# Pairs of heads in one 4 MB tile, and five rows per partition for the weights, in a decode-attention and MLP gradient kernel

## The chip, the cores and the metric

The kernel runs on one core of a Trainium2 chip. The metric is the device time of one execution in microseconds. Times of single instructions, transfers and packets come from one profiled execution; the trace counts from its first instruction.

## The reference

One token (a row of 640) passes a layer norm, then attention over a cache of 8192 positions and a gated MLP in parallel. What is computed is the output and, by the chain rule, the gradients of it against all inputs but one for a given `grad_out`:

```python
xn = layernorm(x)                                   # (1, 640)
q = (xn @ wq).reshape(32, 128)                      # 32 heads of 128
s = einsum("hd,hkd->hk", q, k_cache) * 128 ** -0.5  # k_cache, v_cache: (32, 8192, 128) bf16
p = softmax(s)
o = einsum("hk,hkd->hd", p, v_cache)
out_0 = x + o.reshape(4096) @ wo + (silu(xn @ w1) * (xn @ w3)) @ w2    # F = 1728
# gradients: out_1 dx, out_2 dK, out_3 dV, out_4 dwq, out_5 dwo, out_6 dw1, out_7 dw3, out_8 dw2
```

With one query per head, dV of a head is the outer product of p and a row (wo times grad_out), and dK the outer product of U = p * (v . do - sum) and q. So each head reads K and V of 2 MB each and writes dK and dV of 2 MB each: 268 of the 303.5 MB that move.

## The kernel before

A tile of K or V of one head lies as 128 partitions of 64 positions: `(p j) d -> p (j d)`, 16 KB of consecutive memory per partition. Ten such tiles (`free_slots`, `kv_tiles`) are all the space for K and V. The gradients are written into the tile of the input: `outer_v` puts dV over V, `outer_k` puts dK over K, `store` sends the tile out and hands it back.

All these transfers are issued on SP (SyncE) in the order of the program (`fifo`). A transfer waits on SP for what it needs, and everything behind it on SP waits too. `load_next` takes the next of `pending` (K0, V0, K1, V1 and so on) and the tile that has been free the longest, but only when at least `lag` tiles are free (1 at the start, 3 afterwards), so that the store which last used the tile has some time to finish:

```python
        if not pending or len(free_slots) < lag[0]:
            return
```

It is called after every store and whenever the MLP gives back a tile. Loads and stores of wq, wo and their gradients in groups of four heads go over POOL's queue (q0), those of group 0, of the last group and a few rows of others over SP (q1).

`head(h)` is an order written out by hand. TensorE transposes K in chunks of 8 position rows (`T`, four 128x128 transposes, evicted by ScalarE to a `KT` tile), `Mp` multiplies pairs of chunks with the query spread in `qz`, `ev` evicts the scores, `selm` selects and transposes them into the tile `m`. Then `mx`, `mx_bc`, `expo`, `zsum` and `probs` make the softmax; each is a small step on another engine. The same is done with V (`rdot`, `dsum` make U). `o_sum` and `dq_sum` are weighted sums over V and K on TensorE with the weights spread in `Z`. VectorE writes the outer products of head h-1 while TensorE works on head h: `outers_a(h-1)` at the start of `head(h)` (two halves of dV, its store, the first half of dK), `outers_b(h-1)` after `probs(h)` (the rest of dK, its store). `side_k`, `side_m`, `side_v`, `side_pe1` and others place the work of the groups (`prep_do`, `prep_q`, `fin_wo`, `fin_wq`) between these steps.

Before head 2 the kernel does the MLP (`mlp`, `MLP_AT = 2`). Its weights lie in four of the ten tiles, w1 and w3 as `(ci p) f`, so that a partition holds the rows p, p + 128, ...; four of the five blocks lie in `mA` and `mB`, the fifth in `mC`. The gradients dw1 and dw3 are written over the weights and leave over POOL's queue, and each tile then goes back to `free_slots`. For dx the products of weights and the gradient row (`L657`, `L670`) are summed over columns on TensorE into `dx_acc`.

At the end comes the last group's dwo and dwq, the layer norm's gradient, and out_1, transposed to five rows of 128 and sent in two transfers.

Of the kernel before, what the change touches and what calls it, by code (L numbers as in the profile page):

```python
# [16 lines left out]
P = 128  # L17
# [4 lines left out]
def kernel(  # L22
# [31 lines left out]
    GH = 4  # L54
    NG = H // GH
    GW = GH * DH
    KVN = J * DH
# [16 lines left out]
    kc = A_k_cache.rearrange("b h (p j) d -> (b h) p (j d)", p=P)  # L74
    vc = A_v_cache.rearrange("b h (p j) d -> (b h) p (j d)", p=P)
    dkc = out_2.rearrange("b h (p j) d -> (b h) p (j d)", p=P)
    dvc = out_3.rearrange("b h (p j) d -> (b h) p (j d)", p=P)
    wq_v = A_wq.rearrange("(ci p) n -> p ci n", p=P)
    wo_v = A_wo.rearrange("(h p) c -> p h c", p=P)
    dwq_v = out_4.rearrange("(ci p) n -> p ci n", p=P)  # L80
    dwo_v = out_5.rearrange("(h p) c -> p h c", p=P)
    w1_v = B_w1.rearrange("(ci p) f -> p ci f", p=P)
    w3_v = B_w3.rearrange("(ci p) f -> p ci f", p=P)
    dw1_v = out_6.rearrange("(ci p) f -> p ci f", p=P)
    dw3_v = out_7.rearrange("(ci p) f -> p ci f", p=P)
# [5 lines left out]
    NA = NC - 1  # L91
    NSLOT = 10
    RW = 64
# [22 lines left out]
    free_slots = [kvpool.tile([P, KVN], BF16, name=f"kv{i}", tag=f"kv{i}") for i in range(NSLOT)]  # L116
    kv_tiles = {}
    pending = [("K", h) if k == 0 else ("V", h) for h in range(H) for k in range(2)]

    lag = [1]  # L120

    def load_next():
        if not pending or len(free_slots) < lag[0]:
            return
        kind, h = pending.pop(0)
        t = free_slots.pop(0)
        fifo(t[:], (kc if kind == "K" else vc)[h])
        kv_tiles[(kind, h)] = t
# [5 lines left out]
    mC = free_slots.pop(0)  # L134
    mD = free_slots.pop(0)
    mA = free_slots.pop(0)
    mB = free_slots.pop(0)
    w1a = mA[:, 0:NA * F].rearrange("p (c f) -> p c f", f=F)
    w3a = mB[:, 0:NA * F].rearrange("p (c f) -> p c f", f=F)
    w1b = mC[:, 0:F]  # L140
    w3b = mC[:, F:2 * F]
    w2b = mC[:, 2 * F:2 * F + (NB - NBA) * D].rearrange("p (b c) -> p b c", c=D)
    BC0 = 2 * F + (NB - NBA) * D
    assert BC0 + 2 * F <= KVN
    bc_sb = mC[:, BC0:BC0 + 2 * F].rearrange("p (w f) -> p w f", f=F)
    w2a = mD[:, 0:NBA * D].rearrange("p (b c) -> p b c", c=D)
# [6 lines left out]
    fifo(w1a, w1_v[:, 0:NA, :])  # L153
    fifo(w1b, w1_v[:, NA, :])
    fifo(w3a, w3_v[:, 0:NA, :])
    fifo(w3b, w3_v[:, NA, :])
    for _ in range(2):
        load_next()
# [8 lines left out]
    pm_one = masks[:, 0:2]  # L167
    nc.vector.memset(pm_one[:, 0:1], 1.0)
    nc.vector.memset(pm_one[:, 1:2], -1.0)
    ones_b = pm_one[:, 0:1].to_broadcast([P, P])  # L170
    negones_b = pm_one[:, 1:2].to_broadcast([P, P])
    one_bf = consts.tile([P, 1], BF16, name="one_bf")
    nc.vector.memset(one_bf[:], 1.0)
    eps_t = consts.tile([P, 1], F32, name="eps_t")
    nc.vector.memset(eps_t[:], LN_EPS)
# [18 lines left out]
    DHALF = D // 2  # L194

# [7 lines left out]
    negmean = consts.tile([P, 1], F32, name="negmean")  # L203
    rstd = consts.tile([P, 1], F32, name="rstd")
    x_col = consts.tile([P, NC], F32, name="x_col")
    g_col = consts.tile([P, NC], F32, name="g_col")
    xn_col = consts.tile([P, NC], F32, name="xn_col")
# [12 lines left out]
    ln3 = consts.tile([P, 3], F32, name="ln3")  # L220
    xsum, sumsq, std = ln3[:, 0:1], ln3[:, 1:2], ln3[:, 2:3]
    ps_xg = pst()
    ps_g = pst()
    for ci in range(NC):
        nc.tensor.matmul(ps_xg[:, ci:ci + 1], lhsT=x_row[:, ci * P:(ci + 1) * P], rhs=one_bf[0:1, :],
                         start=True, stop=True)
        nc.tensor.matmul(ps_xg[:, NC + ci:NC + ci + 1], lhsT=g_row[:, ci * P:(ci + 1) * P], rhs=one_bf[0:1, :],
                         start=True, stop=True)
# [6 lines left out]
    nc.vector.tensor_copy(x_col[:], ps_xg[:, 0:NC])  # L235
    nc.vector.tensor_copy(g_col[:], ps_xg[:, NC:2 * NC])
    nc.vector.tensor_reduce(xsum, x_col[:], AX.X, ALU.add)
    nc.tensor.matmul(ps_xg[:, 16:17], lhsT=ones_b, rhs=xsum, start=True, stop=True)
    nc.vector.tensor_scalar(negmean[:], ps_xg[:, 16:17], -1.0 / D, None, ALU.mult)
    nc.vector.scalar_tensor_tensor(xn_col[:], x_col[:], negmean[:], x_col[:], ALU.add, ALU.mult, accum_out=sumsq)  # L240
    nc.tensor.matmul(ps_xg[:, 17:18], lhsT=ones_b, rhs=sumsq, start=True, stop=True)
    nc.scalar.activation(std, ps_xg[:, 17:18], ACTF.Sqrt, bias=eps_t[:], scale=1.0 / D)
    nc.vector.reciprocal(rstd[:], std)
    nc.vector.tensor_scalar(xn_col[:], x_col[:], negmean[:], rstd[:], ALU.add, ALU.mult)
    nc.vector.tensor_copy(xn_col_bf[:], xn_col[:])

    def prep_new(g):
        G_ = grp[g]
        G_["cb"] = wpool.tile([P, 2, GH], BF16, name="cb", tag="cb")
        G_["do"] = wpool.tile([P, GH], F32, name="do_c", tag="do_c")  # L250
        G_["cm"] = wpool.tile([P, 2, 2, GH, 2], BF16, name="cm_g", tag="cm_g")
        G_["od"] = wpool.tile([P, GH, 2], F32, name="od_g", tag="od_g")

    def prep_do(g, hh):
        G_ = grp[g]
        junk = small.tile([P, D], BF16, name="side", bufs=1)
        nc.vector.scalar_tensor_tensor(junk[:], G_["wo"][:, hh, :], 1.0, g_bc[:], ALU.mult, ALU.mult,  # L257
                                       accum_out=G_["do"][:, hh:hh + 1])
        if hh == GH - 1:
            nc.vector.tensor_copy(G_["cb"][:, 1, :], G_["do"][:])  # L260
# [18 lines left out]
    def prep_sel(g, ps):  # L279
        for par in range(2):  # L280
            nc.tensor.matmul(ps[:, par * 2 * GH:(par + 1) * 2 * GH], lhsT=sel[:, par, :],
                             rhs=grp[g]["cb"][:].rearrange("p a h -> p (a h)"), start=False, stop=True,
# [8 lines left out]
    NCH = J // 8  # L291
    QL = NCH - 2
    qz_tiles = []
    for i in range(2):
        qz = consts.tile([P, QL + 4 * QW], BF16, name=f"qz{i}")
        nc.vector.memset(qz[:], 0.0)
        qz_tiles.append(qz)
    P2_1 = consts.tile([P, J, 2], BF16, name="P2_1")
    U2_1 = consts.tile([P, J, 2], BF16, name="U2_1")
    NI = J // 4  # L300
    Z = consts.tile([P, QW - 4 + NI * QW], BF16, name="Z")
    nc.vector.memset(Z[:], 0.0)
    Z_vals = Z[:, QW - 4:].rearrange("p (i n) -> p i n", n=QW)[:, :, 0:4]
    QH = 2 * QW
    selc = consts.tile([P, QH], F32, name="selc")
    for x in range(QW // NCH):
        nc.vector.tensor_copy(
            selc[:, 2 * NCH * x:2 * NCH * (x + 1)].rearrange("p (e o t) -> p o e t", o=2, t=2),
            ident_f[:, 0:QH].rearrange("p (o x e t) -> p x o e t", o=2, e=NCH // 2, t=2)[:, x])

    def new_head(h):
        hd[h] = dict(kt={}, qz=qz_tiles[h % 2])

    def T(h, kind, c):
        W3 = kv_tiles[(kind, h)][:].bitcast(F32).rearrange("p (i w) -> p i w", w=P)
# [5 lines left out]
        hd[h]["kt"][(kind, c)] = KT  # L321

    def Mp(h, kind, c0):
        S_ = hd[h]
# [10 lines left out]
        for par in range(2):  # L335
            for c in (c0, c0 + 1):
                q = QW * (c - c0)
                o = QL + QW * (2 * a + par) - c0
                nc.tensor.matmul(S_[kind][q:q + QW, :], lhsT=S_["qz"][:, o:o + QW], rhs=KTb[c][:, par, :],  # L339
                                 start=(c0 == 0 and par == 0), stop=(c0 == NCH - 2 and par == 1),  # L340
                                 skip_group_check=True)

    def ev(h, kind):
        S_ = hd[h]
# [4 lines left out]
    def selm(h, kind):  # L349
        S_ = hd[h]  # L350
        if kind == "K":
            S_["m"] = ps_m.tile([P, 512], F32, name="m", tag="m")
        b0 = 0 if kind == "K" else J
        XS = S_.pop("xr" + kind)
        for k in range(4):
            nc.tensor.matmul(S_["m"][:, b0:b0 + 4 * J].rearrange("p (x c k t) -> p k x c t", x=4, k=4, t=2)[:, k],  # L356
                             lhsT=XS[0:QH, k, :], rhs=selc[0:QH].rearrange("p (x c t) -> p x c t", x=4, t=2),
                             start=(kind == "K" and k == 0), stop=True, is_transpose=True, skip_group_check=True)
        S_[kind] = S_["m"][:, b0:b0 + J]

    def fill_qz(h):
        g, hh = divmod(h, GH)
        nc.vector.tensor_copy(
            hd[h]["qz"][:, QL:QL + 4 * QW].rearrange("p (a t n) -> p a t n", t=2, n=QW)[:, :, :, 0:2],
            grp[g]["cm"][:, :, :, hh, :].rearrange("p t a m -> p a t m"))

    def rows_pe(h, ps, first):
        g, hh = divmod(h, GH)
        for a in range(2):
            nc.tensor.matmul(ps[:, a * DH:(a + 1) * DH], lhsT=grp[g]["cb"][:, a, hh:hh + 1].to_broadcast([P, P]),  # L370
                             rhs=ident_bf[:], start=(first and a == 0), stop=True, skip_group_check=True)
        hd[h]["ps_r"] = ps

    def rows_act(h):
        qd = small.tile([P, 2, DH], BF16, name="qd")
        nc.scalar.copy(qd[:].rearrange("p a d -> p (a d)"), hd[h].pop("ps_r"))  # L376
        hd[h]["qd"] = qd

    def mx(h):
        S_ = hd[h]  # L380
        S_["mrow"] = small.tile([P, 1], F32, name="mrow")
        nc.vector.tensor_reduce(S_["mrow"][:], S_["K"][:, 0:J], AX.X, ALU.max)  # L382

    def mx_bc(h):
        S_ = hd[h]
        nc.tensor.matmul(S_["m"][:, 2 * J:2 * J + P], lhsT=S_["mrow"][:].to_broadcast([P, P]), rhs=ident_f[:],  # L386
                         start=False, stop=True, is_transpose=True, skip_group_check=True)
# [510 lines left out]
```

## Time and profile before

| | |
|---|---|
| median of 3 runs | 729.37 us (729.15 to 729.87) |
| profiled execution, first to last instruction (span) | 727.5 us |
| median minus span | 1.9 us |
| TensorE / VectorE / ScalarE busy | 603.3 / 459.8 / 376.2 us (83 / 63 / 52%) |
| packets and bytes | 28625, 303.54 MB, 417 GB/s over the span |
| q1 (SP) / q0 (POOL), share of 16 engines | 90.5% / 8.5% |
| mean granted TensorE clock | 0.916 |

The execution's time holds the span and what lies before its first and after its last instruction; the median minus the span stands for that here. The profile's page shows the span in 40 slices, with the busy share of each engine and of the 16 DMA engines in tenths. A packet is what one DMA engine moves at a time: 16 KB for a row of K or V. Lines such as `L318` are lines of the kernel above; `T` is L314 to L321, the outer product L466.

### The profile page before, as it was taken

Reading aid. Unit: us, or ns where it says so; the run is one execution under the profiler, and the core shown is the slowest. Engines: PE = TensorE matmul, PEld = TensorE weight load, DVE = VectorE, ACT = ScalarE, POOL = GpSimd, SP = SyncE. Lnnn points to the kernel's source line nnn. Section 1 sums busy time; section 2 is a strip of 40 time slices with the busy share of each in tenths; the row PEclk is TensorE's granted clock in tenths of the full one; section 3 lists DMA queues with packets and bytes.
Section 4 is the critical chain, followed back from the end, with each engine's and each line's share of the span. In section 5 each row is a group of like instructions: output and inputs, shape, how many; then the busy total and the mean of one; then the engine's idle time right before and its main releaser. Section 6 shows DMA issues by size and latency. Waiting matters only on the chain.

```text
span 727.5 us, 12942 instructions
## 1 busy us (share of the span) xinstructions
PE 603.3 (83%) x5186; PEld 377.1 (52%) x5193; DVE 459.8 (63%) x811; ACT 376.2 (52%) x727; POOL 32.3 (4%) x48
## 2 busy tenths in 40 slices
PE   4989489999899989888897789878796988988930
PEld 2547366665565556555454456445554555545510
DVE  4169646688868776667565756457665666667581
ACT  3640746665666566545454546455463555655510
POOL 0010100000000000000010000000000000000000
PEclk9997799999999999989998989899998999999965
DMA  9999999999999999999999999999999999999995
GB/s 351 400 411 421 428 426 430 427 426 430 420 420 431 430 412 420 426 428 421 420 425 428 430 426 428 420 431 428 421 422 427 429 425 423 425 432 427 426 415 221
DMA packets 28625, 303.54 MB, mean 417 GB/s; under 512 B 3354, under 2 KB 5929, under 8 KB 11924
## 3 DMA queue, kind: packets, MB, share of 16 engines
q1 hardware_dynamic: 22578, 277.75, 90.5%
q0 software_dynamic: 5968, 24.94, 8.5%
q8 instruction: 41, 0.67, 0.4%
q14 instruction: 20, 0.16, 0.1%
q10 hardware_dynamic: 18, 0.01, 0.0%
HBM read 151.34 MB, written 151.34 MB: 416 GB/s over the span
## 4 chain that ended last, share of the span: by engine, by line
DMA 51%; PE 36%; DVE 7%; ACT 2%; issue 1%; SPq 0%; ACTq 0%; DVEq 0%
DMA kv<-in_A_v_cache_dram 20%; PE pT L318 17%; DMA out_dram<-kv 16%; DMA kv<-in_A_k_cache_dram 14%; PE sA L339 5%; PE dA L339 4%; PE X L433 3%; DVE kv L466 3%; PE m L356 2%; DMA wo_g<-in_A_wo_dram 2%; ACT KT L320 1%; PE gu_ps L561 1%; PE pT L266 1%; PE m L400 1%; ACT KT L346 0%
## 5 line engine op out<-in xcount | busy, mean ns | idle before, releaser
L320 ACT COPY KT<-pT 128x512 f32<-128x512 f32 x512 | 288.3, 588 | 227.9 <-PE pT L318 208.6
L318 PE MATMUL pT<-ident_f,kv 128*128 128x128 f32 x2048 | 308.2, 290 | 53.7 <-DMA kv<-in_A_v_cache_dram 24.2
L318 PEld LDWEIGHTS pT<-ident_f,kv 128*128 128x128 f32 x2048 | 237.4, 149 | 146.2 <-PE pT L318 51.8
L466 DVE TENSOR_TENSOR kv<-qd,U 128x4096 bf16<-128x4096 bf16 x64 | 146.0, 2284 | 0.0
L466 DVE TENSOR_TENSOR kv<-qd,P 128x4096 bf16<-128x4096 bf16 x64 | 143.6, 2285 | 0.0
L433 PE MATMUL X<-kv,Z 128*32 128x512 bf16 x1024 | 97.1, 413 | 1.8 <-DVE Z L450 1.8
L339 PE MATMUL dA<-KT,qz 128*32 128x512 bf16 x512 | 84.2, 408 | 0.0
L339 PE MATMUL sA<-KT,qz 128*32 128x512 bf16 x512 | 83.5, 406 | 0.0
L416 DVE SCALAR_TENSOR_TENSOR U<-m,P 128x64 bf16<-128x64 f32 x32 | 7.5, 233 | 87.4 <-PE m L356 87.4
L433 PEld LDWEIGHTS <-Z 128*32 128x32 bf16 x1024 | 33.2, 101 | 35.3 <-issue 8.7
L339 PEld LDWEIGHTS <-qz 128*32 128x32 bf16 x1024 | 29.5, 95 | 40.8 <-issue 38.3
L382 DVE TENSOR_REDUCE mrow<-m 128x1 f32<-128x64 f32 x32 | 7.1, 223 | 68.4 <-PE m L356 68.3
L356 PE MATMUL m<-selc,KT 64*128 64x64 f32 x256 | 30.5, 242 | 10.3 <-ACT KT L346 10.3
L356 PEld LDWEIGHTS m<-selc,KT 64*128 64x128 f32 x256 | 21.5, 144 | 33.2 <-ACT KT L346 22.1
L376 ACT CAST qd<-pT 128x256 bf16<-128x256 f32 x32 | 11.9, 372 | 39.9 <-DVE kv L466 28.7
L389 DVE TENSOR_REDUCE negM<-m 128x1 f32<-128x128 f32 x32 | 9.3, 292 | 33.0 <-PE m L386 33.0
L526 DVE SCALAR_TENSOR_TENSOR wq_g<-wq_g,side 128x512 bf16<-128x512 bf16 x40 | 27.3, 683 | 0.0
L257 DVE SCALAR_TENSOR_TENSOR side<-wo_g,g_bc 128x640 bf16<-128x640 bf16 x32 | 26.2, 819 | 1.3 <-DMA wo_g<-in_A_wo_dram 0.9
L448 DVE SCALAR_TENSOR_TENSOR U<-m,P 128x128 bf16<-128x128 f32 x32 | 11.4, 356 | 16.3 <-PE m L446 16.3
L406 DVE RECIPROCAL rZ<-m 128x1 f32<-128x1 f32 x32 | 5.3, 166 | 24.2 <-PE m L400 24.2
L346 ACT COPY KT<-dA 64x512 f32<-64x512 f32 x32 | 18.6, 582 | 3.7 <-PE dA L339 3.7
L346 ACT COPY KT<-sA 64x512 f32<-64x512 f32 x32 | 18.6, 581 | 2.1 <-PE sA L339 1.9
(162 smaller groups left out, 372.7 us busy)
## 6 DMA issues: line engine op xcount, KB each, us to landing
out_dram<-kv SPq DMA_DIRECT2D x64, 2048.0 KB
kv<-in_A_k_cache_dram SPq DMA_DIRECT2D x32, 2048.0 KB
kv<-in_A_v_cache_dram SPq DMA_DIRECT2D x32, 2048.0 KB
wq_g<-in_A_wq_dram POOLq DMA_DIRECT2D x7, 640.0 KB, 13.4
wo_g<-in_A_wo_dram POOLq DMA_DIRECT2D x7, 640.0 KB, 19.1
out_dram<-wo_g POOLq DMA_DIRECT2D x7, 640.0 KB, 14.4
kv<-in_B_w_dram SPq DMA_DIRECT2D x2, 1728.0 KB
out_dram<-kv POOLq DMA_DIRECT2D x2, 1728.0 KB, 23.5
```

The costliest lines, as they stand in the source:

```text
L257: nc.vector.scalar_tensor_tensor(junk[:], G_["wo"][:, hh, :], 1.0, g_bc[:], ALU.mult, ALU.mult, accum_out=G_["do"][:, hh:hh + 1])
L318: nc.tensor.transpose(pT[:, k * P:(k + 1) * P], W3[:, 4 * c + k, :], ident_f[:])
L320: nc.scalar.copy(KT[:].rearrange("p k w -> p (k w)"), pT[:])
L339: nc.tensor.matmul(S_[kind][q:q + QW, :], lhsT=S_["qz"][:, o:o + QW], rhs=KTb[c][:, par, :], start=(c0 == 0 and par == 0), stop=(c0 == NCH ...
L346: nc.scalar.copy(XS[0:QH].rearrange("p k w -> p (k w)"), S_.pop(kind)[0:QH, :])
L356: nc.tensor.matmul(S_["m"][:, b0:b0 + 4 * J].rearrange("p (x c k t) -> p k x c t", x=4, k=4, t=2)[:, k], lhsT=XS[0:QH, k, :], rhs=selc[0:Q ...
L376: nc.scalar.copy(qd[:].rearrange("p a d -> p (a d)"), hd[h].pop("ps_r"))
L389: nc.vector.tensor_reduce(S_["negM"][:], S_["m"][:, 2 * J:2 * J + P], AX.X, ALU.max, negate=True)
L433: nc.tensor.matmul(xg["X"][q:q + QW, :], lhsT=Z[:, o:o + QW], rhs=W[:, N4 * i:N4 * (i + 1)], start=(slot == 0 and i < 4), stop=(slot == NS ...
L448: nc.vector.scalar_tensor_tensor(S_["U2"][:], S_["V"][:, 0:J].unsqueeze(2).to_broadcast([P, J, 2]), S_["m"][:, OC + NS:OC + NS + 1], S_["P ...
L466: nc.vector.tensor_tensor(dst[:, lo * DH:hi * DH].rearrange("p (j a b) -> p j a b", a=DH // 2, b=2), vec.rearrange("p (a b) -> p a b", b=2 ...
L526: nc.vector.scalar_tensor_tensor(wq_g[:, ci, :], wq_g[:, ci, :], 1.0, dqb, ALU.mult, ALU.mult, accum_out=dxa[:, ci, g:g + 1])
```

## The change

Heads 0, 1, 30 and 31 stay single. Heads 2 to 29 become 14 units of two: K (or V) of both heads is one tile of 4 MB, the first head in partitions 0 to 63, the second in 64 to 127, 32 KB of consecutive memory per partition. There are five tiles of 4 MB instead of ten of 2 MB; a single head takes half of one. One load or store moves a whole pair. All steps of a head are done once per pair, on twice as many columns; matmuls that sum or select over a head's partitions are done per half (`halfsum`, `selm`, `rows_pe`, `mx_bc`). The lag counts in halves: 3 halves free, where a pair needs one whole tile. `load_next` is now called until it has nothing to issue.

w1, w3, dw1 and dw3 lie as `(p ci) f`, five consecutive rows (17,280 bytes) per partition, in two 4 MB tiles with w2; the MLP gives back two tiles instead of four. wq and dwq use the same order of rows. x_col and the other columns follow it, and x goes into `acc` as a row at the start. out_1 is transposed into a row and leaves in one transfer.

```diff
-    KVN = J * DH
+    KVN = 2 * J * DH
+    KVH = J * DH
...
+    units = [(0,), (1,)] + [(h, h + 1) for h in range(2, H - 2, 2)] + [(H - 2,), (H - 1,)]
+    def kv_ap(t, u):
+        heads = units[u]
+        return t[0, heads[0]:heads[0] + len(heads)].rearrange("e (q j) d -> (e q) (j d)", q=P // len(heads))
-    wq_v = A_wq.rearrange("(ci p) n -> p ci n", p=P)
+    wq_v = A_wq.rearrange("(p ci) n -> p ci n", ci=NC)
-    w1_v = B_w1.rearrange("(ci p) f -> p ci f", p=P)
+    w1_v = B_w1.rearrange("(p ci) f -> p (ci f)", ci=NC)
...
-    NSLOT = 10
+    NSLOT = 5
...
     def load_next():
-        if not pending or len(free_slots) < lag[0]:
-            return
-        kind, h = pending.pop(0)
-        t = free_slots.pop(0)
-        fifo(t[:], (kc if kind == "K" else vc)[h])
-        kv_tiles[(kind, h)] = t
+        if not pending:
+            return False
+        kind, u = pending[0]
+        n = len(units[u])
+        spare = [half_of[id(t)] for t, _ in free_half]
+        if 2 * len(free_full) + len(spare) < lag[0] or not (free_full or (n == 1 and free_half)):
+            return False
+        pending.pop(0)
+        t, i, ap = take(n)
+        fifo(ap, kv_ap(A_k_cache if kind == "K" else A_v_cache, u))
+        kv_tiles[(kind, u)] = (t, i, ap)
+        return True
...
-    fifo(w1a, w1_v[:, 0:NA, :])
-    fifo(w1b, w1_v[:, NA, :])
-    fifo(w3a, w3_v[:, 0:NA, :])
-    fifo(w3b, w3_v[:, NA, :])
-    for _ in range(2):
-        load_next()
+    fifo(w1f, w1_v)
+    fifo(w3f, w3_v)
+    load_next()
     lag[0] = 3
...
+    for e in range(2):
+        nc.tensor.matmul(acc[64 * e:64 * (e + 1), 0:DHALF], lhsT=one_bf[0:1, :].to_broadcast([1, 64]),
+                         rhs=x_row[:, e * DHALF:(e + 1) * DHALF], start=False, stop=True, skip_group_check=True)
...
+            for e in range(2):      # selm, for a pair
+                nc.tensor.matmul(
+                    S_["m"][e * HB:(e + 1) * HB, b0:b0 + L.J].rearrange("p (c k t) -> p k c t", k=4, t=2)[:, k],
+                    lhsT=XS[0:QH, k, e * HB:(e + 1) * HB], rhs=selp[0:QH, e, :].rearrange("p (c t) -> p c t", t=2),
+                    start=st_, stop=True, skip_group_check=True)
...
-    def store(kind, h):
-        t = kv_tiles.pop((kind, h))
+    def store(kind, u):
+        t, i, ap = kv_tiles.pop((kind, u))
         if kind == "K":
-            hd.pop(h)
-        fifo((dkc if kind == "K" else dvc)[h], t[:])
-        free_slots.append(t)
-        load_next()
+            hd.pop(u)
+        fifo(kv_ap(out_2 if kind == "K" else out_3, u), ap)
+        give(t, i)
+        while load_next():
+            pass
...
-        FA, FB = 256, 832
+        FA = 192
         for wi in range(2):
...
             for f0 in range(0, F, FA):      # 9 products of 5 x 192 columns (were 7 of 4 x 256 and 3 of 832)
...
+            for ci in range(NC):
+                nc.vector.tensor_scalar(ws[:, ci, :], bc_sb[:, wi, :], xn_col[:, ci:ci + 1], None, ALU.mult)
+            nc.gpsimd.dma_start((dw1_v, dw3_v)[wi], wf)
+            free_full.append((mX, mY)[wi])
+            while load_next():
+                pass
...
+    def outers_a(u):
+        n = len(units[u])
+        for i in range(2 * n):
+            outer_v(u, i)
+        store("V", u)
+        for i in range(n):
+            outer_k(u, i)
...
+    def sides(u):
+        if L.n == 2 and hh == 0 and g > 0:
+            S["m"] += [lambda: fin_od(g - 1)]
+            S["pe"] += [lambda: fin_pe(g - 1)]
+            S["v"] += [lambda: fin_wo(g - 1)]
+            S[10] += [lambda: fin_wq(g - 1, 0)]
+            S[12] += [lambda: fin_wq(g - 1, 1)]
+        if L.n == 2 and hh == 2:
...
+            S[8] += [lambda: prep_q(g + 1), lambda: prep_do(g + 1, 2)]
...
     def head(u):
...
         T(u, "V", 7)
         Mp(u, "V", 4)
+        side("v")
+        for c in range(8, NCH, 2):
+            T(u, "V", c)
+            T(u, "V", c + 1)
+            Mp(u, "V", c - 2)
+            side(c)
...
-    nc.tensor.transpose(ps_o[0:NC, 0:P], fin[:], ident_f[:])
-    nc.vector.tensor_copy(fin_bf[:], ps_o[0:NC, 0:P])
-    for lo, hi in ((0, 4), (4, NC)):
-        nc.scalar.dma_start(out_1.rearrange("a b (c p) -> (a b c) p", p=P)[lo:hi, :], fin_bf[lo:hi, :])
+    for ci in range(NC):
+        nc.tensor.transpose(ps_o[ci // 4][0:1, (ci % 4) * P:(ci % 4 + 1) * P], fin[:, ci:ci + 1], ident_f[:])
+    nc.vector.tensor_copy(fin_v[:, 0:4, :], ps_o[0][0:1, :].rearrange("o (c p) -> o c p", p=P))
+    nc.vector.tensor_copy(fin_v[:, 4:NC, :], ps_o[1][0:1, 0:P].rearrange("o (c p) -> o c p", p=P))
+    nc.scalar.dma_start(out_1.rearrange("a b (q c) -> (a b) q c", q=4), fin_bf.rearrange("p (q c) -> p q c", q=4))
```

## The prediction, made before the changed kernel ran

> **What bounds the kernel now.** I read the page's slices and queues first, then the windows by stage, then the rows of SP, PE and DVE around 120 us.
>
> ```profile
> span 727.5 us, 12942 instructions
> PE   4989489999899989888897789878796988988930
> DMA  9999999999999999999999999999999999999995
> q1 hardware_dynamic: 22578, 277.75, 90.5%
> q0 software_dynamic: 5968, 24.94, 8.5%
> ```
>
> The transfers fill 99% of the span; PE has room in nearly every slice.
>
> ```profile
> 0.00:30.00 30.00, 18.92 (x118) 11.72 (x118) 8.39 (x42) 14.08 (x24) 0.69 (x6) 0.94 0.95 373
> 30.00:60.00 30.00, 26.55 (x295) 18.12 (x296) 19.54 (x26) 13.17 (x28) 3.69 (x6) 0.92 1.01 406
> 60.00:98.00 38.00, 24.76 (x253) 17.94 (x252) 31.50 (x75) 14.29 (x9) 3.75 (x6) 0.77 1.01 426
> 98.00:124.00 26.00, 26.00 (x223) 16.86 (x221) 10.84 (x19) 17.60 (x34) 0.54 (x1) 0.97 1.01 428
> 124.00:142.00 18.00, 17.41 (x157) 11.31 (x158) 12.53 (x19) 11.36 (x25) 0.00 (x0) 1.00 1.01 430
> 683.00:728.00 45.00, 14.41 (x120) 8.55 (x120) 22.58 (x47) 7.29 (x15) 0.00 (x0) 0.66 0.81 334
> ```
>
> The last two columns are DMA share and GB/s. From 30 us on the share is 1.01 until the tail: a hole in the stream adds its whole length to the end. Bytes follow too: 373 x 30 + 406 x 30 + 426 x 38 + 428 x 26 makes 50.7 MB by 124 us.
>
> ```profile
> 107.20 0.33 SPq L105 DMA_DIRECT2D kv<-in_A_v_cache_dram  x1
> 120.41 0.34 SPq L105 DMA_DIRECT2D out_dram<-kv  x1
> 124.47 0.33 SPq L105 DMA_DIRECT2D kv<-in_A_k_cache_dram  x1
> ```
>
> 107.20 is the load of head 5's V, 120.41 the store of head 2's dV. Between them the lag rule finds too few free tiles and nothing is issued on SP; what is queued at 107.20 must last until 120.41, and just does. This is the thinnest place of the stream.
>
> ```profile
> 103.91 0.63 PE L339 MATMUL sA<-KT,qz 128*32 128x512 bf16 x4
> 104.47 1.09 PE L318 MATMUL pT<-ident_f,kv 128*128 128x128 f32 x8
> 105.49 0.63 PE L339 MATMUL sA<-KT,qz 128*32 128x512 bf16 x4
> ```
>
> ```profile
> 89.58 4.16 DVE L657 TENSOR_TENSOR KT<-kv,kv 128x1024 bf16<-128x1024 bf16 x7
> 115.89 4.49 DVE L466 TENSOR_TENSOR kv<-qd,P 128x4096 bf16<-128x4096 bf16 x2
> ```
>
> Two chunks of eight K rows take 105.49 - 103.91 = 1.58 us on PE; an outer product of 32 rows takes 2.2 us on DVE.
>
> **The first 4 MB store.** Followed through the two free lists, SP's order in the new kernel is: K0, V0, K1, V1, the MLP's weights, K2-3; the stores of heads 0 and 1; V2-3, and as the MLP frees its tiles K4-5 and V4-5. Then one whole tile is free, the lag rule asks for two, and the next entry is the store of dV2-3. Ahead of it stands the same work as before: sixteen halves of 2.10 MB (33.6), weights of groups 0 to 2 (3.9), MLP weights in and gradients out (13.3), 50.8 MB, so the stream runs dry near 124.5 us. But that store comes later than 120.41:
> - MLP: before, w3's products run 4.16, then four scalings 2.41, then three products 1.19, and PE starts head 2 at 98.3. New: nine products of 960 columns (0.65 each) come before any scaling, so from 89.6 they end near 95.5 and PE starts near 96.1: -2.2.
> - K: eight more chunks before the scores are complete, four steps of 1.58: +6.3. V likewise: +6.3.
> - Group 1's q is prepared inside this pair. Head 3, which has this work, takes 9.06 us from K's eviction to V's (122.13 to 131.19), head 2 takes 7.20: +1.9.
> - Sixteen more weighted-sum matmuls: +1.05. More of the small matmuls of selection, maximum and sums, wider P and U, a second copy into Z (rows of 0.2 to 0.4): between 0 and 2, taken as +1.0.
> - Two more outer products before the store: +4.5.
>
> Sum 139.2. At the start SP issues at 0.74 and packets begin at 1.78, so the stream resumes near 140.3. **The hole is 140.3 - 124.5 = 15.8 us**, 3 either way. Behind that store on SP wait the load of K6-7 and all that follows; POOL has nothing to move then.
>
> **After the hole.** A pair moves four times 4.19 MB and 1.3 MB of weights: 42 us at 428 GB/s. With V landing at 0, dK of the pair before must be issued by 19.6 and this pair's dV by 42. At head 21 V lands at 475.1, dK's second half starts at 481.96, dV at 490.44: 6.9 and 15.4. For a pair: 6.9 + 1.0 + 4.5 = 12.4, and 15.4 + 6.3 + 2.0 + 1.9 + 8.9 = 34.5. Both have 7 us to spare, so I expect no second hole.
>
> **The tail.** Before, V31 lands at 683.3 and the end comes 44.2 later. New, V28-29 lands at 0 and V31 some 40.7 later, the same stores are left, so the stream ends near 84.9. DVE meanwhile: outer products of the pair from 21 (head 2's 11.4 from V's first chunk, plus 6.3, 2.0 and 1.3 for group 6's matmuls) take six times 2.2, with three steps of dwq at 1.05; each of the heads 30 and 31 then adds 3.8 from maximum to P, its outer products and 1.2 to 4.7 for U. dK31 is issued near 70. From there 9.9 to dwq's store (702.8 to 712.7), then 7.5 for the packets of its last 68 rows, which the trace shows on about four engines: 87.6. DVE is last by 2.7, not DMA; between 0 and 6, taken as **+2.5**.
>
> **The rows.** The two queue lines (22578 a + 277.75 b = 0.905 x 16 x 727.5; 5968 a + 24.94 b = 0.085 x 16 x 727.5) give b = 37.0 us per MB and a = 11 ns per packet. The packet records give 46 ns for 1024 bytes and 611 for 16384, 9 beyond the slope, and neighbours overlap by 4 to 5. After the hole 52 transfers of 4 MB have 128 data and 16 completion packets fewer, nine per engine: 468 in all, 2.1 us at 4.5 ns, 5.1 at 11. No 32 KB packet is in the trace; cut in two it would bring 0, and disturbed like the mean 16 KB packet (617 for 611) it would cost 1%, +6. I take **-2.4**, nearest to the records. w1, w3 and gradients lose 1408 packets (1280 to 256, 640 to 256), 0.4 to 1 us, all ahead of the hole, which swallows it.
>
> The Trainium skill ("DMA: Bandwidth & Descriptors", Anatomy of one DMA) gives a transfer some 2 us fixed beside its bytes; 56 transfers fewer would be 112 us gained. The trace disagrees: q1 is 100.1% busy from 128 to 150 us, with six K and V issues in it.
> The same page (Where 436 GB/s comes from) puts the ceiling at 435.2 GB/s; an estimate by it, from 428, is at most 10 us gained behind the hole.
>
> **The rest.** wq keeps its 1 KB pieces. x added to acc at the start lies under the wait for wo_g (until 13.06). out_1 takes four more transposes (0.37), one more copy (0.28) and one issue less (2.43 for two): about 0.6, done near 714 while dwq's packets run to 726; without that cover +0.6.
>
> **Sum.** The median 729.37 stands 1.9 above the profiled span. 729.4 + 15.8 + 2.5 - 2.4 = **745.3 us**.
>
> **Rivals.**
> *No hole* (not slower): if dV2-3 were issued before about 127, only packets count: 729.4 - 2.4 = 727.0. For it: the bytes ahead are equal, and a slower start would let them last longer. Against: 12.6 us of added chunks stand before the store. It decides once hole and tail together fall below the packets' 2.4. 6%.
> *A hole in every pair*: if the chain from V's landing is 8 us longer than worked out, each of 13 pairs loses a microsecond or more: 758 and up. For: low clock after waits (0.66 at the end), DVE's work at group ends. Against: head 21's rows hold such waits already. 12%.
> *A longer first pair*: every open term at its upper end, hole 19, tail 6, rows 0: 754. 8%.
>
> **How the numbers follow.** Forecast 74%: hole 13 to 18, tail 0 to 6, rows -5 to 0, from 738 to 751. The range 737 to 752 leaves out no hole and most of the last two rivals. About 0.2%, 1.5 us, is what a measurement of this kernel can tell from no change: faster 4%, within it 2%, slower 94%, the 6% being *no hole*.
>
> **What would show it.** Right: q1 near 14,000 packets; DMA digits below 9 around 125 to 140 us and 9 elsewhere; the first 4 MB store issued near 139, with nothing on SP for some 25 us; a share of 1.01 from there to the tail. Wrong: DMA at 9 throughout the first 200 us; dips every 42 us; or full stretches below 425 GB/s, in which long rows cost.

## The result and the profile after

The changed kernel takes 768.08 us in the median of four runs (767.55 to 772.99), the kernel before 729.62 (729.15 to 730.24) beside it: a ratio of 1.054 (1.051 to 1.057), 38.5 us more, where the forecast was 16 more. The page of the changed kernel, profiled in an execution of 767.55 us:

```profile
span 765.8 us, 13167 instructions
PE   4989499969797697958898679779888787897851
DMA  9999994599999999999999999999999999999974
q1 hardware_dynamic: 13458, 277.75, 87.1%
q0 software_dynamic: 5552, 24.94, 8.2%
```

The hole stands in the seventh and eighth slice, and q1 has 9,100 packets fewer. Everywhere else the digit is 9, but a 9 begins at 90%. The windows by stage tell more; the last three columns are the clock, the DMA share and GB/s:

```profile
98.00:124.00 26.00, 26.00 (x207) 16.09 (x205) 10.48 (x26) 16.09 (x31) 0.53 (x1) 1.00 0.99 414
124.00:142.00 18.00, 18.00 (x197) 11.21 (x194) 9.89 (x12) 10.12 (x22) 0.00 (x0) 1.00 0.02 6
142.00:270.00 128.00, 105.40 (x961) 63.13 (x960) 75.10 (x104) 61.40 (x119) 4.03 (x5) 0.92 1.00 412
270.00:480.00 210.00, 173.61 (x1557) 103.54 (x1557) 125.50 (x180) 99.45 (x195) 9.83 (x12) 0.90 1.00 414
480.00:683.00 203.00, 168.58 (x1477) 102.00 (x1476) 121.21 (x162) 98.21 (x192) 8.23 (x11) 0.92 1.00 415
683.00:766.00 83.00, 50.88 (x427) 31.33 (x424) 55.15 (x92) 24.35 (x50) 1.58 (x2) 0.76 0.84 345
```

Before, the three long windows moved 424, 425 and 426 GB/s at a share of 1.01:

```profile
142.00:270.00 128.00, 121.23 (x1073) 75.16 (x1074) 95.78 (x165) 78.95 (x160) 5.71 (x7) 0.99 1.01 424
270.00:480.00 210.00, 180.70 (x1509) 111.63 (x1511) 129.48 (x211) 111.62 (x222) 10.54 (x13) 0.92 1.01 425
480.00:683.00 203.00, 173.29 (x1453) 105.80 (x1451) 129.12 (x212) 107.88 (x214) 7.36 (x9) 0.93 1.01 426
```

Now they move 412 to 415, in stretches that the page calls full. Three landmarks of the records split the loss. The packets of the first pair's dV start at 143.5, where the stream before had reached the same byte at 124.6: +18.9. From there to V31's landing takes 568.1 (to 711.6) against 558.7 (to 683.3): +9.4. From there to the end takes 54.2 against 44.2: +10.0. Together 38.3.

**The hole.** SP's timeline around the first pair:

```profile
112.09 0.33 SPq L107 DMA_DIRECT2D kv<-in_A_v_cache_dram  x1
142.68 0.34 SPq L107 DMA_DIRECT2D out_dram<-kv  x1
143.18 0.33 SPq L107 DMA_DIRECT2D kv<-in_A_k_cache_dram  x1
```

Nothing is issued for 30.6 us; the queue is empty from about 124.4. TensorE meanwhile is busy for all 18.00 us of the window from 124 to 142, at a granted clock of 1.00: the stream waits for the first pair's own work.

**The long stretch.** What SP waits for has changed sides. Before, its waits (line, releaser: us, times, longest) were above all for a landed store, and less for VectorE's outer product: stores were ready early and the queue was full.

```profile
SPq L105 <- DMA out_dram<-kv: 470.8, 55, 14.7
SPq L105 <- DVE kv L466: 83.4, 13, 12.9
```

Now:

```profile
SPq L107 <- DVE kv L564: 505.6, 27, 30.2
SPq L107 <- DVE wo_g L621: 127.2, 8, 21.1
SPq L107 <- DMA out_dram<-kv: 44.8, 3, 29.2
```

The first two lines, 632.8 us, are waits for VectorE. Nearly every store is issued at the moment its last outer product is done, and often little is left in the queue: by the packet records 11 of the 49 pair transfers that start between 142 and 683 either start within 0.7 us of the end of their issue or follow one that does. The usual 32 KB packet takes 1213 ns, exactly the two 16 KB packets of 611 less their overhead that the forecast counted on, but the mean is 1251. Counting what K and V packets take above 1213 or 611 ns gives a time per DMA engine, "slow packets" below: 16.2 us between 142 and 683, before 4.7. Those 11 transfers hold 9.2 of the 16.2, about as much in the ones that start so soon as in the ones that follow.

**The tail** is told with the steps below.

### The profile page after: what moved, and what is told of

Its sections match the earlier page's. It is cut to its first block, busy times and chain, and to the rows that moved or that the text cites. A ratio compares the mean times of both kernels' runs of the same rounds, so it can differ in the third digit from the quotient of the medians.

```text
span 765.8 us, 13167 instructions
## 1 busy us (share of the span) xinstructions
PE 613.8 (80%) x5423; PEld 374.5 (49%) x5423; DVE 452.0 (59%) x699; ACT 351.1 (46%) x667; POOL 30.8 (4%) x46
## 3 DMA queue, kind: packets, MB, share of 16 engines
q1 hardware_dynamic: 13458, 277.75, 87.1%
## 4 chain that ended last, share of the span: by engine, by line
DMA 49%; PE 41%; DVE 6%; ACT 2%; issue 1%; SPq 0%; DVEq 0%; ACTq 0%
DMA kv<-in_A_v_cache_dram 47%; PE pT L369 20%; PE dA L391 6%; DVE kv L564 3%; PE sA L391 3%; DMA wo_g<-in_A_wo_dram 2%; PE X L525 2%; PE dx_acc L745 1%; PE m L416 1%; ACT kv L729 1%; PE pT L291 1%; PE gu_ps L660 1%; PE m L411 1%; PE acc L227 1%; PE m L473 1%
## 5 line engine op out<-in xcount | busy, mean ns | idle before, releaser
L525 PE MATMUL X<-kv,Z 128*32 128x512 bf16 x1024 | 87.7, 449 | 1.8 <-DVE Z L484 1.8
L505 DVE SCALAR_TENSOR_TENSOR U<-m,P 128x128 bf16<-128x128 f32 (+1 forms) x18 | 5.2, 289 | 133.6 <-PE m L416 124.8
L451 DVE TENSOR_REDUCE sc<-m 128x1 f32<-128x128 f32 (+1 forms) x18 | 5.0, 276 | 85.9 <-PE m L416 70.5
L391 PEld LDWEIGHTS <-qz 128*32 128x32 bf16 x1024 | 29.6, 95 | 43.1 <-issue 42.2
L416 PEld LDWEIGHTS m<-selp,KT 64*64 64x64 f32 x448 | 15.8, 138 | 9.4 <-issue 8.7
L416 PE MATMUL m<-selp,KT 64*64 64x32 f32 x448 | 18.9, 225 | 0.0
L443 ACT CAST qd<-pT 128x256 bf16<-128x256 f32 x18 | 6.7, 373 | 22.5 <-PE pT L436 16.1
L609 POOL DMA_DIRECT2D out_dram<-wq_g x10 | 8.2, 821 | 218.8 <-DVE wq_g L629 218.8
L629 DVE TENSOR_SCALAR wq_g<-side,cols 128x512 bf16<-128x512 bf16 x40 | 15.1, 377 | 1.4
L729 ACT CAST kv<-pT 128x512 bf16<-128x512 f32 x6 | 13.9, 2654 | 3.9 <-PE pT L725 3.9
L461 DVE TENSOR_REDUCE sc<-m 128x1 f32<-128x64 f32 (+1 forms) x18 | 4.3, 240 | 19.1 <-PE m L459 19.1
```

The source lines that it names most:

```text
L416: nc.tensor.matmul(S_["m"][e * HB:(e + 1) * HB, b0:b0 + L.J].rearrange("p (c k t) -> p k c t", k=4, t=2)[:, k], lhsT=XS[0:QH, k, e * HB:(e ...
L525: nc.tensor.matmul(xg["X"][q:q + QW, :], lhsT=Z[:, o:o + QW], rhs=W[:, N4 * i:N4 * (i + 1)], start=(first and i < 4), stop=(last and i >= ...
L609: nc.gpsimd.dma_start(dst[lo:hi], t[lo:hi])
L629: nc.vector.tensor_scalar(wq_g[:, ci, :], dqb, xn_col[:, ci:ci + 1], None, ALU.mult)
L729: nc.scalar.copy(bc_sb[:, wi, 0:NBA * P].rearrange("p (f b) -> p b f", b=NBA)[:, b0:b0 + bn, :], pb[:, 0:bn * P].rearrange("p (b f) -> p b ...
```

## The experiments

The theories after the result were **D**, the queue runs nearly dry at each store because a pair's stores come late and large; **R**, rows of 32 KB move slower; **P**, the order on TensorE delays the stores. Where no range is given, a kernel ran once.

*Rows of 16 KB.* Each 4 MB transfer becomes two, all else as changed.

```diff
-        fifo(ap, kv_ap(A_k_cache if kind == "K" else A_v_cache, u))
+        src = kv_ap(A_k_cache if kind == "K" else A_v_cache, u)
+        for i0 in range(0, n * KVH, KVH):
+            fifo(ap[:, i0:i0 + KVH], src[:, i0:i0 + KVH])
...
```

> The changed kernel, but each 4 MB transfer is issued as two of 2 MB with 16 KB rows, one right behind the other; waits and tiles as in the changed kernel. Theory R (rows of 32 KB are slow in themselves: mean packet 1251 ns where 1213 is the usual one): packets return to 611 to 617 ns, the stretch 270 to 683 us rises from 414 to about 425 GB/s, 768 falls to 756 to 758. Theory D (the queue is nearly dry before every store, so the 16 engines start in step and disturb each other; the row length has no part): still 412 to 416 GB/s, 768 to 771. The hole at 125 to 143 us stays in both.

759.4 us (757.3 to 762.1), ratio 1.039 (1.036 to 1.042); 419 to 422 GB/s, slow packets 10.8. Between the two theories, and less clean than meant: the first half of a store waits for its own outer products only, so dV2-3 begins at 138.73 and not at 142.68. Both the rows and that head start can have won the 9 us; the copies and the half stores below take them one at a time.

*Half of the outer products* of the pairs are left out, so that half of their dK and dV isn't computed and stores come some 4.5 us sooner.

```diff
-        for i in range(2 * n):
+        for i in range(2):
             outer_v(u, i)
...
```

> The changed kernel without half of the outer products of the pairs (two of four for dV, two of four for dK; the rest of each tile goes out as it came in), so stores are ready 4.4 us earlier and the queue never runs dry behind the first hole. Theory D: 422 to 427 GB/s from 270 to 683 us, hole 4.4 shorter, 768 falls by 10 for the rate, 4 for the hole and some 7 in the tail, to 745 to 750. Theory R: the rate stays near 414, only hole and tail shrink: 756 to 759.

752.4 us (749.3 to 753.7); dV2-3 issued at 137.69, 418 to 421 GB/s with 32 KB rows, slow packets 12.3. This too lies between the theories: stores that are ready earlier (and half of VectorE's work on them) bring back 15.7 us, a part of it through the higher rate, though the rows are as long as they were.

*Lag 2 once*, when the MLP gives back its second tile, so that K6-7 is loaded without waiting for dV2-3.

```diff
             free_full.append((mX, mY)[wi])
+            lag[0] = 3 - wi
...
```

> The changed kernel, but the lag is 2 halves once, when the MLP gives back its second tile, so that the load of K6-7 goes out about 15 us before the store of dV2-3. If the missing free tile makes the hole: it shrinks from 19 us to two pieces of 4 to 6 us, 768 falls to 759 to 763. If the hole has another cause (the store's own lateness alone, with nothing else to move): no change.

767.0 us (765.5 to 769.9), no change, the second of the two cases. 124 to 142 now moves 217 GB/s, but 142 to 270 only 390: the idle time moved behind the early load. The late stores, not the free tile, set the stream.

*Single heads*: every head its own unit in half a tile, and all the rest of the change kept (five rows per partition, two 4 MB tiles for the MLP, the row of out_1).

```diff
-    units = [(0,), (1,)] + [(h, h + 1) for h in range(2, H - 2, 2)] + [(H - 2,), (H - 1,)]
+    units = [(h,) for h in range(H)]
...
```

> The changed kernel with all heads single (10 halves, lag 3 halves, 16 KB rows, the group work placed as in the kernel before); five rows per partition for the weights, x at the start and the row for out_1 stay. Both theories: 728 to 730, the rate 424 to 427 GB/s, no hole at 125 us: the whole loss lies in the pairs. If the weights' layout or the end has a part in the loss, it stays above 731.

732.3 (730.5 to 735.8), ratio 1.002 (1.001 to 1.004). Its windows:

```profile
142.00:270.00 128.00, 122.52 (x1043) 79.98 (x1045) 87.13 (x144) 72.58 (x153) 5.68 (x7) 0.96 1.01 422
270.00:480.00 210.00, 200.19 (x1711) 130.24 (x1705) 141.72 (x231) 119.31 (x249) 10.63 (x13) 0.96 1.01 424
```

So all but some 2 us of the loss lies in the pairs. The time stays above the 731 named, so those 2 us belong to the rest of the change.

*Theory P: the next unit's K after the weighted sums.* In the changed kernel the first transposes of the next pair's K stand ahead of V's last products, and PE waits there for a K that lands late:

```profile
209.60 1.94 PE L369 MATMUL pT<-ident_f,kv 128*128 128x128 f32 x8 [3.88 <-DMA kv<-in_A_k_cache_dram]
215.66 0.30 DVE L505 SCALAR_TENSOR_TENSOR U<-m,P 128x128 bf16<-128x128 f32 x1 [9.66 <-PE m L416]
```

V6-7 had landed at 188.1, U comes 27.6 later, and dV6-7 is issued at 226.39, 38.3 after the landing instead of the 34.5 of the forecast. The edit moves those transposes behind `dsum` and `dq_sum`:

```diff
-        if pre:
-            T(u + 1, "K", 0)
-            T(u + 1, "K", 1)
         Mp(u, "V", NCH - 2)
...
         dq_sum(u)
+        if pre:
+            for c in range(4):
+                T(u + 1, "K", c)
+            Mp(u + 1, "K", 0)
...
```

> The changed kernel, but the first four K chunks of the next unit are transposed after the weighted sums of this one, not before its last V chunk, so a late K load no longer stands in front of U and of the next store on PE. Theory P (in the steady stretch the next K's landing, 21 us after V's, sets when dV is ready, which is why stores come 1 to 3 us before the queue is dry instead of 7): the store of a pair comes 34 to 36 us after its V's landing instead of 38 to 42, the hole is 1 us shorter, the rate 418 to 420, 768 falls to 759 to 763. If the margin is lost elsewhere (DVE, evictions): 766 to 770.

767.8 us (765.3 to 769.4): P missed. dV in the steady stretch is now issued 29 to 35 us after its V's landing, where the changed kernel takes 34 to 41, even sooner than expected. But dK's stores then come 20 to 33 us behind dV's instead of 16 to 22, dV2-3 comes at 145.30, and the time is the same. The lateness changes its store.

*Query rows late*: `rows_pe` and `rows_act` of the next unit move behind `dsum`, away from the wait for `qd`'s buffer in the tail.

```diff
-            rows_pe(u + 1, pst()[:, 0:2 * DH], True)
-            rows_act(u + 1)
...
         dsum(u)
+        if nxt:
+            rows_pe(u + 1, pst()[:, 0:2 * DH], True)
+            rows_act(u + 1)
```

> The changed kernel with rows_pe and rows_act of the next unit placed after dsum, not before the last V chunk. Theory Q (in the tail, ScalarE's eviction into qd waits for the pair's second outer products of dK, since there are two qd buffers, and holds back U of head 30): the last stretch, from V31's landing to the end, falls from 53 us by 3 to 5, time 763 to 765. Without Q: 767 to 769.

763.7 us (762.6 to 764.8), ratio 1.046 (1.043 to 1.049), as expected, and the tail's 3.68 us wait is gone:

```profile
715.77 0.37 ACT L443 CAST qd<-pT 128x256 bf16<-128x256 f32 x1 [0.40 <-PE pT L436]
```

That the sum fits is in part luck: from V31's landing (713.1) to the end it takes 47.7 us, 6.4 less than before the edit and not 3 to 5, and the stretch ahead of it is longer, with slow packets of 19.2 us and 410 to 414 GB/s.

*Transfers alone.* K and V go through the tiles to dV's and dK's places and the other inputs to other outputs; nothing is computed (in all kernels of this kind). One has ten 2 MB tiles and 16 KB rows, the other five 4 MB tiles and 32 KB rows, both with a lag that keeps the queue full.

```diff
+    while held:
+        k, hs, t = held.pop(0)
+        nc.sync.dma_start(view((out_2, out_3)[k], hs), t[:])
+        free.append(t)
+        if todo and len(free) >= lag:
+            load()
```

> The transfers alone: K and V of each head are loaded into ten tiles of 2 MB (16 KB rows) and sent out as dK and dV, in the order and with the lag (3) of the kernel before; no computation, the other outputs are copies of inputs of the same shape at the end. Both theories: packets of 611 to 617 ns, 425 to 430 GB/s in the middle.

> The same with five tiles of 4 MB for two heads (32 KB rows), a load when two tiles are free; no computation, the other outputs are copies of inputs. Theory R (long rows are slow in themselves): packets of 1240 to 1260 ns, 412 to 418 GB/s in the middle though nothing computes. Theory D (near-dry queue): 1213 to 1220 ns and 428 to 433 GB/s.

16 KB rows: 682.7 us (682.5 to 682.9), 430 to 431 GB/s, 611 ns in the median and 612.7 in the mean. 32 KB rows: 683.5 us (682.7 to 684.3), as a whole no shorter, in their window (DMA share and GB/s last):

```profile
100.00:300.00 200.00, 0.00 (x0) 1.00 1.00 433
```

Mean 1218. R falls for a full queue: there the long rows move at 432 to 433 GB/s, some 0.4% faster, what the forecast's -2.4 us said.

*The same with a queue that runs dry*, each tile loaded again as soon as it is stored.

```diff
-        if todo and len(free) >= lag:
+        if todo and len(free) >= 1:
```

> Transfers alone: K and V are copied to the outputs through five 4 MB tiles with 32 KB rows, no engine computes, and each tile is loaded again as soon as it is stored, which lets the queue run dry around each store. With a full queue (lag two) the same copies took 683.5 us, 432 to 433 GB/s, 32 KB packets 1213 ns in the median and 1218 in the mean. Theory D (a queue that has just run dry hands out long rows that take longer, compute or not): mean of the 32 KB packets 1235 to 1270, most of the excess in the two transfers after each dry moment; rate 405 to 425, span 690 to 720. Theory C (it is the engines' work on SBUF or the small transfers beside that makes long rows slow): mean at or under 1222, only the empty time itself is lost.

> The same copies with 16 KB rows through ten 2 MB tiles, each loaded again as soon as it is stored. With a full queue: 682.7 us, 430 to 431 GB/s, packets 611 in the median and 612.7 in the mean. Theory D: mean 618 to 640, and as it runs dry twice as often (64 stores instead of 32) the span is longer than with 32 KB rows, 700 to 760. Theory C: mean at or under 614.

```profile
100.00:300.00 200.00, 0.00 (x0) 1.00 0.92 364
```

That is the window with 32 KB rows; 313 with 16 KB. Means 1311 and 692, spans 777.5 and 881.0: D's side, and stronger than expected. SP's issues of a load:

```profile
315.65 0.33 SPq L64 DMA_DIRECT2D kv<-in_A_k_cache_dram  x1
338.88 0.33 SPq L64 DMA_DIRECT2D kv<-in_A_v_cache_dram  x1
```

They are 23.2 us apart here, 23.1 in the mean, for a round of 8.39 MB (a load and a store), which takes 19.4 at 432 GB/s. So one dry moment costs 3.7 us, with 16 KB rows the same (13.4 for 9.7). About 1.9 us of it is empty (2.1 with 16 KB rows); the rest is in slow packets. With 32 KB rows these are the first of each engine, mostly 1400 to 2200 ns, some 0.6 us of a round, and those where all engines change from the load to the store at once, 10 us into a round (1900 to 2400 ns), some 1.1 us. A full queue has 1.1 us of slow packets in 500. The Trainium skill ("DMA: Bandwidth & Descriptors", Anatomy of one DMA) gives a transfer that GpSimd issues about 2 us that don't depend on its size. K and V are issued by SP. Behind a full queue no run here shows such a cost; at a dry moment the empty part is near it, and the slow packets come on top.

*Half stores*: from "query rows late", each pair's dV and dK leave in two halves, the first as soon as half of the outer products are done; loads stay 4 MB.

```diff
         for i in range(2 * n):
             outer_v(u, i)
+            if i == n - 1 and n == 2:
+                half_store("V", u, 0)
...
```

> The changed kernel with the query rows of the next pair after the V sums (as in the run with rows late, 763.7 us), and each pair's dV and dK stored in two halves of 16 KB rows, the first as soon as the first two of its four outer products are done; loads stay 4 MB with 32 KB rows. dV's first half leaves 4.5 us earlier, dK's first half some 16 to 20 us earlier than dK as a whole; tiles come free when they did. Theory N (the lost rate comes from a queue that is nearly dry at each store): hole some 4 us shorter, no dry moments after it, 421 to 425 GB/s from 270 to 683, 745 to 755 us. Theory L (the long rows of the loads, or the engines' work beside them, cost the rate): hole 4 us shorter, but 414 to 418 GB/s, 757 to 762 us.

759.7 us (758.2 to 762.6), ratio 1.040 (1.037 to 1.044):

```profile
270.00:480.00 210.00, 173.07 (x1558) 108.35 (x1558) 124.90 (x179) 98.57 (x195) 9.83 (x12) 0.91 1.01 416
480.00:683.00 203.00, 169.81 (x1496) 104.11 (x1494) 117.71 (x167) 96.86 (x189) 8.98 (x11) 0.90 1.00 412
```

The first store is issued at 136.35 for 140.74, 4.4 us sooner, as much as the whole gain of 4.0. The share is 1.00 to 1.01 in nearly every 10 us after the hole, and still the packets are slow: 16.1 us, of which 6.1 lie in the 20 us from each of six stores of dwq on (0.5 to 1.3 each). Theory N, that the nearly dry queue is all, falls with it. L fits the time, but not the copies above. "Rows of 16 KB", whose loads too are in 16 KB rows, has 10.8 us of slow packets against these 16.1, so in the kernel's own order of transfers a part of the long rows is not excluded.

*What stands beside the transfers.* The copies with a full queue again: with the groups' wq and wo loaded and stored through POOL's queue (32 and 16 KB rows), with TensorE, ScalarE and VectorE busy on tiles of their own, and with both. The group traffic:

```diff
+            nc.gpsimd.dma_start(dwq_v[0:126, :, g * GW:(g + 1) * GW], wq_g[0:126])
+            nc.sync.dma_start(dwq_v[126:P, :, g * GW:(g + 1) * GW], wq_g[126:P])
+            nc.gpsimd.dma_start(dwo_v[:, g * GH:(g + 1) * GH, :], wo_g[:])
```

> Transfers alone with 32 KB rows and lag two as before (433 GB/s, packets 1213 ns in the median, 1218 in the mean), and beside them the group traffic of the kernel: wq and wo groups loaded and stored through GpSimd's queue once per four heads, two rows of dwq through SP's. Theory S (small transfers beside long rows make these slow): mean of the 32 KB packets 1235 to 1260, the excess in the 20 us from each group's stores on. Theory E (the engines' work does it) or dry queue alone: 1215 to 1225.

> The same group traffic beside 16 KB rows (alone 611 ns in the median, 612.7 in the mean). Theory S with the row length deciding: mean at most 616, half the excess per byte of the 32 KB run or less. Theory S without it (small transfers cost both alike): 617 to 630, the same time per group as with 32 KB rows. Theory E: at most 614.

> 32 KB rows and lag two, no group traffic, but TensorE transposes, ScalarE copies and VectorE products of the kernel's shapes on tiles of their own for most of the span. Theory E: mean of the 32 KB packets 1230 to 1260 while the engines are busy, rate at or under 425 GB/s. Theory S: at most 1222, rate 430 to 433.

> Both beside the 32 KB rows: the group traffic and the busy engines. Theory S: as with the group traffic alone, within 8 ns. Theory E: as with the busy engines alone. If neither alone makes the packets slow and both together do (mean over 1235), it is the pairing; if even both stay under 1225, what is left is the coupling of loads and stores to the computation, that is when each is issued.

Mean of the K and V packets in ns: 1229.6 with the group traffic (between the ranges named), 618.8 for 16 KB rows with it, 1218.7 with busy engines, 1229.8 with both. The window of the third:

```profile
100.00:300.00 200.00, 200.00 (x1294) 135.74 (x1294) 197.07 (x87) 189.56 (x324) 0.00 (x0) 1.00 1.00 432
```

PE, DVE and ACT are busy for 95% and more of those 200 us and the rate stays 432. So the engines' work on tiles of their own doesn't slow the packets. The group traffic does, at either row length (slow packets 5.5 and 4.7 us from 100 to 600, against 1.1 and 0.5 without it; 425 to 428 GB/s). That is about what the kernel before has, 4.7 us, and not the 16.2 of the changed one.

*No dwq stores*: the half-store kernel without the stores of dwq for all groups but the last; that part of one output is not written.

```diff
-            store_group(g, dwq_v[:, :, g * GW:(g + 1) * GW], wq_g, 1 <= g <= 5)
+            if g == NG - 1:
+                store_group(g, dwq_v[:, :, g * GW:(g + 1) * GW], wq_g)
```

> The kernel with half stores, with the stores of dwq left out for all groups but the last (4.5 MB less, 10.5 us at 426 GB/s; that part of one output is not written). Theory W (the dwq stores within the pairs' order of stores and loads make the packets slow): slow packets fall from 16 to 6 us or less between 142 and 683, 32 KB packets to 1230 or less in the mean, 422 to 427 GB/s, 735 to 742 us. Theory O (the order and the bunching of pair stores and loads do it by themselves): 14 to 16 us of slow packets, mean about 1250, 748 to 752 us.

743.4 us in one run; slow packets 11.0, 419, 425 and 416 GB/s. Between the theories: the time fell 16.3 us, 10.5 of it bytes, and slow packets by 5.1. Of what is left, 1.8 us follow the hole, and 2.5 lie in a spell from 600 to 660 in which the share falls to 0.93.

## Why the prediction was wrong, step by step

The direction and the place of the hole were right. All three terms of the sum were too small, the second by most; of the signs of being wrong, "full stretches below 425 GB/s" is what came, though long rows cost nothing in the copies with a full queue.

**Hole: 15.8 forecast, 18.9 measured.** The dry moment was right (124.5 for about 124.4), the store later than forecast by 3.5 (142.68 for 139.2). One entry of the list failed, the MLP:

```profile
94.73 5.20 DVE L742 TENSOR_TENSOR KT<-kv 128x960 bf16<-128x960 bf16 x9
100.38 1.98 PE L369 MATMUL pT<-ident_f,kv 128*128 128x128 f32 x16
```

I let w3's products start at 89.6, where they start before. But w1's round is of the same new form and ends at 94.81. PE starts the pair at 100.38, not at 96.1. From there to the store it takes 42.3, the forecast 43.1: the chunks, group 1's q, the small steps and the outer products held as a sum. That TensorE has room in nearly every slice is not so here: before as after, it is busy for all 26.00 us from 98 to 124.

**After the hole: -2.4 forecast, +9.4 measured.** This is the term that failed most. The price of a long packet was right (1213 ns, and the copies gain 0.4%). "Both have 7 us to spare" was not. dK's chain held (12.5 from V6-7's landing to dK4-5's issue, 12.5 to 14.6 in all, forecast 12.4), dV's did not: 34 to 41, 38 in the mean, for 34.5, with K's landing between, a wait that the forecast didn't price; with the next K moved away (theory P) it took 29 to 35. With a slack of a few us there is no second hole to be seen in the digits, yet the queue is dry or nearly so at 11 transfers, and slow packets make 11.5 us more than before; with the -2.4 that is 9.1 of the 9.4. The bound of +6 for disturbed rows was too near: it took the disturbance of a queue that is always full.

**Tail: +2.5 forecast, +10.0 measured.** The outer products of the last pair start 21.0 after V28-29's landing at 668.92, as forecast. dK31 is issued at 745.7, 76.8 after it, forecast 70:

```profile
713.31 0.37 ACT L443 CAST qd<-pT 128x256 bf16<-128x256 f32 x1 [3.68 <-DVE kv L564]
716.62 0.23 DVE L505 SCALAR_TENSOR_TENSOR U<-m,P 128x64 bf16<-128x64 f32 x1 [2.31 <-PE m L411]
```

`qd` has two buffers. The eviction of the next head's rows waits until the pair's last outer product has read the old one (708.73 plus 4.49), and head 30's U waits behind it. "Query rows late" takes that wait away, and dK31 then comes 71.6 after V28-29's landing, near the 70: the wait was most of this error. Behind dK31 the first dwq store comes 7.5 later (9.9 forecast), but the end another 12.5 after it, where I counted 7.5: its second half is issued only at 758.57. (70, 9.9 and 7.5 add up to 87.4, not to the 87.6 of the forecast, which changes nothing.)

**What held.** q1 has 13,458 packets, near the 14,000 named. The rest cost nothing: out_1's row leaves at 758.90 under dwq's packets though its copies took 1.56 and 0.59, where I had one more of 0.28. "Single heads" shows the rest of the change near zero: 1.6 us at 732.3 for 730.7. Of the rivals, *a hole in every pair* came closest: its time holds (758 and up), and dV's chain was longer, by 4 us in the mean and not 8; what came was a nearly dry queue and no visible hole in every pair.

**Open.** In the changed kernel 9.2 of the 16.2 us of slow packets lie in transfers at dry or nearly dry moments, and the dry copies show that such moments make packets slow without any computing. That they are the cause of the whole excess is not shown: in the half-store kernel, whose queue is hardly dry, the slow packets are still 16.1 us. 5 of these go with the dwq stores, although beside a full stream of the same rows all of the group traffic costs some 0.7 us per group. Why the pairs' order of stores and loads makes them dearer, and what part the long rows have in it, no run here settles. No version tried beats the kernel before.

## What to carry to other kernels

Doubling a transfer that also is a unit of work lengthened the time from its landing until it can be stored (V's landing to the end of dV's outer products: 19.8 us at head 21 before, 34 to 41 for a pair), while the tiles in flight were halved. In a kernel bound by transfers, what is still queued at each store is the quantity to forecast, and a slack of a few microseconds is not "hidden". Read what the issuing queue waits for: here the stream was full while that was a landed transfer, and when it became the last compute step the rate fell, even with every digit a 9. When one round of a repeated step changes its form, move every round before it as well.

## What the runs showed of the hardware

- In the copies without computing, a queue that runs dry for a moment costs 3.7 us at either row length: about 2 empty, the rest in slow packets after the restart and, more of it, at the next change from load to store (up to 2400 ns for the usual 1213).
- With a full queue, rows of 32 KB move at 432 to 433 GB/s, of 16 KB at 430 to 431.
- TensorE, VectorE and ScalarE at 95% and more, on tiles of their own, leave the transfers at 432 GB/s.
- Small transfers, nearly all on another queue, make the large packets slow, by some 0.7 us for each group's 2.6 MB, whatever the row length (5.5 us less the 1.1 of the copy alone with 32 KB rows, 4.7 less 0.5 with 16 KB, in 500 us with six groups).
